# A gated mix of windowed attention and a spatial-gating MLP: where the passes over o, the chunks of wo and VectorE's work for both are issued in the mixing

## The chip, the core and the metric

The kernel runs on one core of a Trainium2 chip. A core has TensorE (PE: matmuls into PSUM), VectorE (DVE), ScalarE (ACT), GpSimd (POOL) and SyncE (SP), each with its own in-order stream of instructions; they meet at semaphores. Data lies in SBUF (128 partitions), matmuls accumulate in eight PSUM banks of 128 x 512 float32, and DMA queues move data between SBUF and memory. SP's queue issues nearly all transfers here; ScalarE's own queue issues a few. The metric is device microseconds of one execution of the whole kernel: the median of several runs, 682.94 us before the change.

## The reference

One input x (2048 x 1024, bf16) goes through two branches, which a per-row gate mixes:

```python
def _A_ref(x, wqkv, wo):          # H = 32 heads of 32, window W = 8, dilation 2
    qkv = (x @ wqkv).reshape(B, S, 3, H, Dh).transpose(2, 0, 3, 1, 4)
    ...
    logits = jnp.einsum('bhsd,bhswd->bhsw', q, kg) * scale
    logits = jnp.where(mask[None, None, :, :], logits, -1000000000.0)
    attn = _softmax(logits, axis=-1)
    o = jnp.einsum('bhsw,bhswd->bhsd', attn, vg)
    return o.transpose(0, 2, 1, 3).reshape(B, S, D) @ wo

def _B_ref(x, w_in, w_sp, b_sp, w_out):
    z = _gelu(jnp.einsum('bsd,df->bsf', x, w_in))
    z1 = z[..., :Fh].copy()
    z2 = _layernorm(z[..., Fh:], axis=-1)
    g = jnp.einsum('ts,bsf->btf', w_sp, z2) + b_sp[None, :, None]
    return jnp.einsum('bsf,fd->bsd', z1 * g, w_out)

g = _sigmoid((x * gate_w).sum(-1, keepdims=True))
return g * _A_ref(x, A_wqkv, A_wo) + (1 - g) * _B_ref(x, ...)
```

S = 2048, D = 1024, Fh = 1792. Each row of the attention looks at 8 earlier rows, two apart, so the attention is elementwise work on VectorE; the projections, the spatial product with w_sp (2048 x 2048) and the products with wo and w_out are matmuls on TensorE.

## The kernel before

The order of every engine's instructions is written out by hand. A small planner, `beat`, keeps a modelled clock of TensorE: `beat.run(cols)` advances `beat.now` as matmuls are issued, and functions put into its heap with `beat.at(t, fn)` are issued once that clock has passed t, wherever the code then is between two products. Whatever `fn` emits lands at that place in its engine's stream, ahead of all that the code emits later. `beat.vector` is a modelled clock of VectorE.

The stages of TensorE, in order: transposes and projections (q, k, v for eight groups of four heads; z2), z1, then the **mixing** (g = w_sp times the normalised z2, line 858 on), then the product with wo and the product with w_out. VectorE does the windowed attention group by group meanwhile (`attention_steps`), well into the mixing.

**The mixing** is 16 groups (`g_group(n)`, u = n // 2 is a block of 256 rows, n % 2 a half of the columns). Each replaces eight block products by seven on sums and differences of blocks. Two PSUM banks accumulate, and a third, a "seed" bank, is forked from the first with ScalarE. In the order of issue on TensorE:

1. product 1 into `pa`; ScalarE **forks** `pa` into a seed bank (`fork`, L856)
2. product 2 into `pd`; ScalarE copies it out (`keep`, L842: p5)
3. product 3 onto `pa`, which needs the fork's reading to be over; copy out (L844: u2)
4. product 4 onto the seed bank; ScalarE writes it to g (L874)
5. product 5 onto `pa`, which needs the u2 copy; copy out (L844: u3). Then `y_norm(n - 1)`: two passes of absolute sums over the last group's y on ScalarE (L669), which wait for VectorE's product with z1 of that group. VectorE adds p5 and u3 (L848)
6. product 6 onto `pd`, which needs the p5 copy; VectorE adds u2 (L848)
7. product 7 onto `pa`, which needs the u3 copy; ScalarE adds the bias (L883). VectorE multiplies g by z1 (L884)

Behind every even group VectorE scales the next block's rows of w_sp (`scale_rows`, L577) and forms their sums (L581, L582); half a microsecond later on the planner's clock `y_finish` scales y of the block before (L674 to L683), and SP stores it (L625).

Beside this run preparations for the product with wo. The matmuls take float16 with power-of-two scales, which need absolute sums:
- `o_norm(g)` (L483): one ScalarE pass over the 128 x 2048 tile `obuf` of the attention group's result, **in place**, so it follows `store_o`, the DMA that reads `obuf` (L428). The last one, in `attended`, writes elsewhere.
- `wo_norm(m)` (L643): one ScalarE pass over a chunk of wo (128 x 768), then the issue of the next chunk's load on ScalarE's own queue (L639), as there is one chunk buffer. Eleven chunks.
- `w_total`, `w_power`, `o_total`, `o_power` (L648 to L659, L486 to L498): small VectorE steps that turn the sums into powers of two, with one tiny matmul each (L655, L492).
- `wo_scale`, `wo_sum` (L513, L518) and `heads_sums(u)` (L503 to L507): VectorE scales wo and the transposed heads of o and forms their sums.

All of these were put into the planner's heap with times of their own. Before the first group three matmuls write the two seed banks (`rest`, L827), so that later products may accumulate onto what ScalarE puts there.

Of the kernel before, what the change touches and what calls it, by code (L numbers as in the profile page):

```python
# [10 lines left out]
F32 = mybir.dt.float32  # L11
# [4 lines left out]
P = 128  # L16
S = 2048
D = 1024
KT = D // P
# [10 lines left out]
ZC = 448  # L30
# [31 lines left out]
def kernel(  # L62
# [367 lines left out]
    def attention_steps(t):  # L430
        beat.at(t - 8.0, lambda: load_qk(0))
        beat.at(t - 7.9, lambda: load_v(0))
        for g in range(NG):
# [8 lines left out]
            if g == 0:  # L442
                t += 5.0
            else:
                for took, fn in pv_steps(g - 1, 0) + pv_steps(g - 1, 1):
                    yield t, took, fn
                t = beat.vector
                beat.at(t + 1.0, lambda g=g: load_v(g))
                beat.at(t + 1.5, lambda g=g: store_o(g - 1))
                beat.at(t + 10.0, lambda g=g: o_norm(g - 1, obuf))  # L450
# [6 lines left out]

    def attended():
# [5 lines left out]
        beat.at(t + 6.0, o_total)  # L464
        beat.at(t + 9.0, o_power)
        plan_heads(0, t + 5.0, 3.0, t + 16.0)
        plan_heads(1, t + 11.0, 3.0)
        for m in range(4):
            beat.at(t + 10.5 + 1.0 * m, lambda m=m: wo_scale(m))
            beat.at(t + 17.5 + 1.5 * m, lambda m=m: wo_sum(m))  # L470
# [50 lines left out]
    prep = {"at": 1e12, "normed": 0, "done": False, "attended": False, "heads": 0}  # L521
# [303 lines left out]
    rest = [seeded.tile([P, 512], F32, name="rest", tag="sd") for _ in range(2)]  # L825
    for r in (0, 1, 0):
        nc.tensor.matmul(rest[r][:], ident[:], mask[:], start=True, stop=True)  # L827
# [31 lines left out]
    def g_group(n):  # L859
# [7 lines left out]
        product(pa, v.a11, b11, f0, f1, True)  # L867
        pb = fork(pa, ZC, lo)
        product(pd, v.s1, t1, f0, f1, True)
# [4 lines left out]
        nc.scalar.copy(g[:, 0, 0], pb[:, 0:ZC])  # L874
        product(pa, v.s3, t3, f0, f1, False)
# [9 lines left out]
        beat.on_vector(1.1)  # L885
        if n + 2 < 2 * NU:
            soon(("z1", n + 2), lambda: load_z1(n + 2))
# [28 lines left out]
    for m in range(11):  # L916
        beat.at(beat.now + 12.0 + 8.0 * m, lambda m=m: wo_norm(m))
    beat.at(beat.now + 3.0, lambda: load_wo_chunk(0))
    beat.at(beat.now + 98.0, w_total)
    beat.at(beat.now + 106.0, w_power)  # L920
    for n in range(2 * NU):
# [16 lines left out]
        if n == 2 * NU - 3:  # L938
            beat.at(beat.now + 0.5, lambda: heads_sums(1))
            plan_heads(2, beat.now + 1.0, 3.0, beat.now + 13.0)  # L940
            plan_heads(3, beat.now + 7.0, 3.0, beat.now + 2 * 7 * KT * ZC * BEAT + 0.5)
    assert prep["attended"]
# [173 lines left out]
```

## Time and profile before

| | |
|---|---|
| median of 3 runs | 682.94 us (681.83 to 683.23) |
| the profiled execution | 681.58 us, span 679.8 us |
| TensorE matmuls busy | 669.3 us |
| VectorE busy | 550.2 us |
| ScalarE busy | 393.9 us |
| the mixing on TensorE | from 368.31 us (group 0) to about 542.7 us |

Rows of a timeline are: start in us from the span's start, duration in us, engine, line of the kernel, operation, what it writes and reads, how many in a row, and in brackets the idle time just before it with what ended it. A matmul's duration reaches from its start to its modelled end, past the start of the next one, so distances are measured from start to start. In a list of waits a row is: who waited, for whom, and then us in total, times, longest us. ACTq and SPq are the queues on which an engine issues transfers.

### The profile page before, as it was taken

The page shows a single profiled execution, that of the slowest core. Times are in us where ns is not written, and L with a number is a line of the kernel's source. Part 1 is how long each engine was busy: PE and PEld are TensorE (multiplying, and loading weights), DVE is VectorE, ACT ScalarE, POOL GpSimd, SP SyncE. Part 2 cuts the span into 40 slices and gives each one's busy share as a digit, 9 for nine tenths or more (in the row PEclk, how much of TensorE's full clock was granted, in tenths as well). Part 3 has the DMA queues.
Part 4 walks back from the last instruction along what each step waited for, and adds up shares of the span by engine and source line. Part 5 has one row for each costly group of instructions (what it writes and reads, how often), then busy time and mean ns, then how long its engine had stood idle before and what let it go on. Part 6 is the DMA issues. An engine that isn't in the chain of part 4 may idle for free. (4 is left out here: it accounts for less than half of the span.)

```text
span 679.8 us, 9533 instructions
## 1 busy us (share of the span) xinstructions
PE 669.3 (98%) x3590; PEld 391.8 (58%) x3590; DVE 550.2 (81%) x628; ACT 393.9 (58%) x736; POOL 13.1 (2%) x23
## 2 busy tenths in 40 slices
PE   9999999999999999999999999989999999999997
PEld 4577788888875555555554555544555444444443
DVE  0009799999999999999999999979956988945745
ACT  4445667665646888858963666655564564522121
POOL 1000000000000000013100000000000000000000
PEclk9999999999999999999999999999999999999999
DMA  8999769998759760437754856494679599385211
GB/s 233 176 232 231 215 183 272 241 259 215 200 121 267 280 199 13 185 102 213 272 170 159 181 144 179 114 273 119 151 209 262 124 254 264 81 171 142 60 63 62
DMA packets 230734, 123.92 MB, mean 182 GB/s; under 512 B 191008, under 2 KB 217248, under 8 KB 230688
## 3 DMA queue, kind: packets, MB, share of 16 engines
q1 hardware_dynamic: 229104, 121.21, 68.1%
q10 hardware_dynamic: 1584, 2.10, 1.1%
q8 instruction: 28, 0.46, 0.3%
q14 instruction: 18, 0.15, 0.1%
HBM read 63.97 MB, written 37.82 MB: 150 GB/s over the span
## 5 line engine op out<-in xcount | busy, mean ns | idle before, releaser
L832 PE MATMUL ps<-arena 128*128 128x448 f16 (+1 forms) x1296 | 264.8, 363 | 4.5 <-ACT seed L856 4.4
L832 PEld LDWEIGHTS <-arena 128*128 128x128 f16 x1512 | 147.7, 98 | 159.6 <-issue 5.7
L713 PEld LDWEIGHTS <-arena 128*128 128x128 bf16 x1024 | 141.6, 138 | 25.6 <-issue 0.8
L713 PE MATMUL ps<-arena 128*128 128x384 bf16 x768 | 130.4, 326 | 0.4 <-DMA arena<-in_A_wqkv_dram 0.4
L374 DVE TENSOR_TENSOR arena<-arena 128x8192 bf16<-128x8192 bf16 x16 | 70.8, 4422 | 46.4 <-DMA arena<-k_d 46.2
L377 DVE TENSOR_TENSOR arena<-arena 128x4096 bf16<-128x4096 bf16 (+1 forms) x64 | 77.6, 1213 | 2.0
L351 PE MATMUL ps<-arena 128*128 128x448 bf16 (+1 forms) x384 | 76.8, 353 | 0.3 <-ACT arena L338 0.3
L351 PEld LDWEIGHTS <-arena 128*128 128x128 bf16 x512 | 49.9, 98 | 46.8 <-ACT arena L338 0.4
L814 PEld LDWEIGHTS <-arena 128*128 128x128 bf16 x512 | 50.0, 98 | 46.6
L814 PE MATMUL ps<-arena 128*128 128x448 bf16 x384 | 75.4, 352 | 0.0
L407 DVE TENSOR_TENSOR arena<-arena,att_A 128x8192 bf16<-128x8192 bf16 x16 | 70.7, 4421 | 0.2
L721 ACT CAST arena<-ps 128x384 bf16<-128x384 f32 x84 | 38.9, 483 | 41.4 <-PE ps L713 37.5
L832 PE MATMUL seed<-arena 128*128 128x448 f16 (+1 forms) x216 | 47.8, 363 | 0.0
L713 PE MATMUL sd<-arena 128*128 128x384 bf16 x256 | 46.8, 326 | 0.0
L357 ACT ACTIVATE arena<-ps 128x448 bf16<-128x448 f32 x48 | 26.1, 546 | 21.7 <-PE ps L351 21.2
L413 DVE TENSOR_TENSOR arena<-arena 128x4096 bf16<-128x4096 bf16 x16 | 36.6, 2290 | 0.4
L1047 ACT ACTIVATE arena<-ps,omr 128x512 f32<-128x512 f32 x24 | 16.5, 687 | 32.4 <-PE ps L832 32.4
L844 ACT ACTIVATE arena<-ps,bt 128x448 f32<-128x448 f32 x32 | 20.3, 633 | 25.4 <-PE ps L832 25.0
L816 ACT ACTIVATE arena<-ps 128x448 bf16<-128x448 f32 x48 | 24.9, 550 | 16.3 <-PE ps L814 14.9
L990 DVE SCALAR_TENSOR_TENSOR arena<-seed,omr,arena 128x512 bf16<-128x512 f32 x8 | 6.0, 751 | 34.5 <-PE seed L832 34.5
L669 ACT ACTIVATE arena<-arena 128x896 bf16<-128x896 bf16 x32 | 30.3, 946 | 3.9 <-DVE arena L884 3.4
L547 ACT ACTIVATE arena<-arena 128x2048 bf16<-128x2048 bf16 x16 | 30.8, 1925 | 0.0
(144 smaller groups left out, 628.5 us busy)
## 6 DMA issues: line engine op xcount, KB each, us to landing
arena<-in_B_w_sp_dram SPq DMA_DIRECT2D x16, 512.0 KB, 5.1
arena<-k_d SPq DMA_DIRECT2D x8, 960.0 KB, 6.6
arena<-v_d SPq DMA_DIRECT2D x8, 960.0 KB, 6.7
z_d<-arena SPq DMA_DIRECT2D x16, 448.0 KB, 2.8
arena<-z_d SPq DMA_DIRECT2D x16, 448.0 KB, 3.9
y_d<-arena SPq DMA_DIRECT2D x16, 448.0 KB, 3.8
arena<-in_A_wqkv_dram SPq DMA_DIRECT2D x24, 256.0 KB, 5.3
arena<-in_B_w_in_dram SPq DMA_DIRECT2D x6, 896.0 KB, 7.7
```

The source lines that it names most:

```text
L351: nc.tensor.matmul(ps[:, 0:N], xT[:, kt, i * P:(i + 1) * P], w2[:, kt, ZC * c:ZC * c + N], start=(kt == 0), stop=(kt == KT - 1))
L357: nc.scalar.activation(z2[:, i, ZC * c:ZC * (c + 1)], ps[:, 0:ZC], ACT.Gelu_apprx_tanh, accum_out=s1[:, 4 * i + c:4 * i + c + 1])
L374: TT(prod.rearrange("p (w j c) -> p w j c", w=W, j=8, c=C), in0, in1, ALU.mult)
L377: return lambda: TT(pv[:, :, 0:half], pv[:, :, 0:half], pv[:, :, half:2 * half], ALU.add)
L407: TT(prod.rearrange("p (w j d h) -> p w j d h", w=W, j=8, d=DH, h=HG), in0, in1, ALU.mult)
L413: return [(4.4, mul), (2.3, lambda: TT(p3[:, 0:4, :], p3[:, 0:4, :], p3[:, 4:8, :], ALU.add)), (1.2, lambda: TT(p3[:, 0:2, :], p3[:, 0:2, ...
L547: nc.scalar.activation(waste, slot, ACT.Abs, accum_out=l1[:, a:a + 1])
L669: nc.scalar.activation(waste, g_ring[n % 4][:, r], ACT.Abs, accum_out=yl[:, k:k + 1])
L713: nc.tensor.matmul(ps[:, 0:3 * C].rearrange("p (t c) -> p t c", t=3), lhsT, wgt[:, 0:3, kt, :], start=(kt == 0), stop=(kt == KT - 1))
L721: nc.scalar.copy(st[:, j % 4, :], ps[:, 0:3 * C])
L814: nc.tensor.matmul(ps[:, 0:ZC], xT[:, kt, i * P:(i + 1) * P], w1[:, kt, :], start=(kt == 0), stop=(kt == KT - 1))
L832: nc.tensor.matmul(ps[:, 0:c1 - c0], w[:, k, :], v[:, k, c0:c1], start=(first and k == 0), stop=(k == K - 1), skip_group_check=True)
```

## The change

Nothing is computed differently and no instruction of an engine is added or taken away; what changes is where they are issued.

- `o_norm` of attention groups that finish in the mixing goes into a list `beside_fork`, and is issued right behind a group's fork, the first one whose time is past (12 us behind its step). Outside the mixing it stays in the heap, with 17 instead of 10 us.
- The `wo_norm` chunks go into `beside_copy`: at most one per group, right behind the copy of product 4 (L874).
- `o_total`, `o_power`, `w_total`, `w_power`, `wo_scale`, `wo_sum`, `heads_sums(0)` and `heads_sums(1)` go into `behind_mult`, a list with a time and a cost each, from which a group takes steps behind its product with z1 (L884), up to 5.0 us of cost (7.4 from group 13 on).
- `heads_sums(2)` and `(3)` stay in the heap with other times.
- The three `rest` matmuls come behind product 1 of group 0 instead of ahead of it.

```diff
@@ -447,7 +447,10 @@
                 t = beat.vector
                 beat.at(t + 1.0, lambda g=g: load_v(g))
                 beat.at(t + 1.5, lambda g=g: store_o(g - 1))
-                beat.at(t + 10.0, lambda g=g: o_norm(g - 1, obuf))
+                if prep["mixing"]:
+                    beside_fork.append((t + 12.0, lambda g=g: o_norm(g - 1, obuf)))
+                else:
+                    beat.at(t + 17.0, lambda g=g: o_norm(g - 1, obuf))
             yield t, 2.3, soft_b
             t = beat.vector
         for took, fn in pv_steps(NG - 1, 0) + pv_steps(NG - 1, 1):
@@ -455,19 +458,27 @@
         t = beat.vector
         beat.at(t + 1.0, attended)
 
+    beside_fork, beside_copy, behind_mult = [], [], []
+
+    def spare(queue):
+        if queue and queue[0][0] <= beat.now:
+            queue.pop(0)[1]()
+
     def attended():
         store_o(NG - 1)
         load_wo()
         o_norm(NG - 1, reg(A_OFF + 8192, 2048).rearrange("p (j c) -> p j c", j=NJ))
         prep["attended"] = True
         t = max(beat.now, beat.vector)
-        beat.at(t + 6.0, o_total)
-        beat.at(t + 9.0, o_power)
-        plan_heads(0, t + 5.0, 3.0, t + 16.0)
+        plan_heads(0, t + 5.0, 3.0)
         plan_heads(1, t + 11.0, 3.0)
+        behind_mult.append((t + 4.0, 0.4, o_total))
+        behind_mult.append((t + 12.0, 0.9, o_power))
         for m in range(4):
-            beat.at(t + 10.5 + 1.0 * m, lambda m=m: wo_scale(m))
-            beat.at(t + 17.5 + 1.5 * m, lambda m=m: wo_sum(m))
+            behind_mult.append((t + 11.0, 0.75, lambda m=m: wo_scale(m)))
+        behind_mult.append((t + 15.0, 2.45, lambda: heads_sums(0)))
+        for m in range(4):
+            behind_mult.append((t + 17.0, 1.25, lambda m=m: wo_sum(m)))
 
     def load_heads(u, r):
         a = 2 * u + r
@@ -518,7 +529,7 @@
         TT(out_, a, b, ALU.subtract)
         beat.on_vector(1.25)
 
-    prep = {"at": 1e12, "normed": 0, "done": False, "attended": False, "heads": 0}
+    prep = {"at": 1e12, "normed": 0, "done": False, "attended": False, "heads": 0, "mixing": False}
 
     def vector_steps(t):
         for item in attention_steps(t):
@@ -822,9 +833,12 @@
                                        ap=[[FH, P], [P * FH, 4], [1, ZC]]), z1s)
     assert prep["done"]
     beat.lead = MIX_LEAD
-    rest = [seeded.tile([P, 512], F32, name="rest", tag="sd") for _ in range(2)]
-    for r in (0, 1, 0):
-        nc.tensor.matmul(rest[r][:], ident[:], mask[:], start=True, stop=True)
+    prep["mixing"] = True
+
+    def wake_seeded():
+        rest = [seeded.tile([P, 512], F32, name="rest", tag="sd") for _ in range(2)]
+        for r in (0, 1, 0):
+            nc.tensor.matmul(rest[r][:], ident[:], mask[:], start=True, stop=True)
 
     def product(ps, w, v, c0, c1, first):
         K = v.shape[1]
@@ -865,13 +879,17 @@
         now(("z1", n), ("y", u - 2))
         pa, pd = [psum.tile([P, 512], F32, name="ps", tag="ps") for _ in range(2)]
         product(pa, v.a11, b11, f0, f1, True)
+        if n == 0:
+            wake_seeded()
         pb = fork(pa, ZC, lo)
+        spare(beside_fork)
         product(pd, v.s1, t1, f0, f1, True)
         p5 = keep(pd, None)
         product(pa, v.s2, t2, f0, f1, False)
         u2 = keep(pa, lo)
         product(pb, v.a12, b21, f0, f1, False)
         nc.scalar.copy(g[:, 0, 0], pb[:, 0:ZC])
+        spare(beside_copy)
         product(pa, v.s3, t3, f0, f1, False)
         u3 = keep(pa, hi)
         if n > 0:
@@ -883,6 +901,10 @@
         nc.scalar.activation(g[:, 1, 0], pa[:, 0:ZC], ACT.Identity, bias=hi)
         TT(g, g, z, ALU.mult)
         beat.on_vector(1.1)
+        room = 5.0 if n < 13 else 7.4
+        while behind_mult and behind_mult[0][0] <= beat.now and room > 0:
+            room -= behind_mult[0][1]
+            behind_mult.pop(0)[2]()
         if n + 2 < 2 * NU:
             soon(("z1", n + 2), lambda: load_z1(n + 2))
 
@@ -914,10 +936,10 @@
     for n in range(2):
         load_z1(n)
     for m in range(11):
-        beat.at(beat.now + 12.0 + 8.0 * m, lambda m=m: wo_norm(m))
+        beside_copy.append((beat.now + 10.0, lambda m=m: wo_norm(m)))
     beat.at(beat.now + 3.0, lambda: load_wo_chunk(0))
-    beat.at(beat.now + 98.0, w_total)
-    beat.at(beat.now + 106.0, w_power)
+    behind_mult.append((beat.now + 115.0, 0.5, w_total))
+    behind_mult.append((beat.now + 122.0, 0.6, w_power))
     for n in range(2 * NU):
         u, fb = n // 2, n % 2
         t = beat.now
@@ -936,10 +958,12 @@
                 fn()
             beat.on_vector(2.8)
         if n == 2 * NU - 3:
-            beat.at(beat.now + 0.5, lambda: heads_sums(1))
-            plan_heads(2, beat.now + 1.0, 3.0, beat.now + 13.0)
-            plan_heads(3, beat.now + 7.0, 3.0, beat.now + 2 * 7 * KT * ZC * BEAT + 0.5)
-    assert prep["attended"]
+            behind_mult.append((0.0, 2.45, lambda: heads_sums(1)))
+            plan_heads(2, beat.now + 1.0, 3.0, beat.now + 2 * 7 * KT * ZC * BEAT + 0.5)
+            plan_heads(3, beat.now + 7.0, 3.0, beat.now + 2 * 7 * KT * ZC * BEAT + 3.5)
+    assert prep["attended"] and not beside_fork and not beside_copy
+    while behind_mult:
+        behind_mult.pop(0)[2]()
 
     t = beat.now
     beat.at(t + 5.0, lambda: y_norm(2 * NU - 1))
```

In the built program the first `o_norm` of the mixing, which was put into the heap ahead of the mixing, moves from group 0 (behind L874) to group 1 (behind the p5 copy, L842); the next one moves from between L669 and L883 of group 7 to right behind the fork of group 8; the last one stays behind the fork of group 12. A chunk stands behind L874 in each of groups 1 to 11. `w_total` is issued behind group 10's L884, `w_power` behind group 11's, `o_total` behind group 12's; `o_power`, `wo_scale`, `heads_sums(0)` and the first `wo_sum` behind group 13's; the other three `wo_sum` and `heads_sums(1)` behind group 14's; `heads_sums(2)` and `(3)` behind group 15's. The order on SP and GpSimd is the same as before.

## The prediction

> **What bounds the kernel now.** I read the page's busy list first, then the list of waits of TensorE, then TensorE's timeline through the mixing, then the timelines of ScalarE and VectorE around each place where TensorE stood.
>
> ```profile
> PE 669.3 (98%) x3590; PEld 391.8 (58%) x3590; DVE 550.2 (81%) x628; ACT 393.9 (58%) x736; POOL 13.1 (2%) x23
> ```
> ```profile
> PE ps L832 <- ACT seed L856: 4.4, 2, 3.4
> ```
>
> TensorE is the bound: 98% busy, and its two waits on the fork (L856) are the only large ones in the mixing. A change that adds and removes no matmul, like this one, can only move such waits. The timeline gives their true size, since a stall is the distance of two starts beyond the work between them:
>
> ```profile
> 365.51 1.68 PE L814 MATMUL sd<-arena 128*128 128x448 bf16 x8
> 367.02 0.38 PE L827 MATMUL rest<-mask,ident 128*128 128x512 bf16 x1
> 367.88 0.59 PE L827 MATMUL rest<-mask,ident 128*128 128x512 bf16 x2 [0.48 <-ACT arena L816]
> 368.31 4.70 PE L832 MATMUL ps<-arena 128*128 128x448 f16 x24
> 372.84 1.68 PE L832 MATMUL seed<-arena 128*128 128x448 f16 x8
> 374.36 9.42 PE L832 MATMUL ps<-arena 128*128 128x448 f16 x48
> 383.62 1.68 PE L832 MATMUL seed<-arena 128*128 128x448 f16 x8
> ...
> 394.21 1.68 PE L832 MATMUL seed<-arena 128*128 128x448 f16 x8
> ...
> 404.80 1.68 PE L832 MATMUL seed<-arena 128*128 128x448 f16 x8
> ...
> 448.69 7.73 PE L832 MATMUL ps<-arena 128*128 128x448 f16 x40
> 459.80 1.67 PE L832 MATMUL ps<-arena 128*128 128x448 f16 x8 [3.38 <-ACT seed L856]
> ...
> 526.44 7.73 PE L832 MATMUL ps<-arena 128*128 128x448 f16 x40
> 535.16 1.67 PE L832 MATMUL ps<-arena 128*128 128x448 f16 x8 [1.00 <-ACT seed L856]
> ```
>
> From one seed row to the next (383.62 to 394.21) a group of seven products takes 10.59 us, so a product takes 1.513. I write P1 to P7 for a group's products; the seed row is P4. Measured with that:
> - Before P1 of group 0: three wake-up matmuls at 0.215 each (367.88 to 368.31 are two) would let P1 start at 367.02 + 0.65 = 367.67; it starts at 368.31. **0.64 us.**
> - Group 0 behind P4: 383.62 - 374.36 = 9.26 against 6 x 1.513 = 9.08. **0.18 us**, hidden inside a busy row.
> - P3 of group 8: 448.69 + 5 x 1.513 = 456.26, but it starts at 459.80. **3.54 us.**
> - P3 of group 15: 526.44 + 7.57 = 534.01, but it starts at 535.16. **1.15 us.**
>
> Together 5.51 us; that is the most that the change can win here. What held ScalarE in group 8 stands in its timeline:
>
> ```profile
> 455.38 1.91 ACT L483 ACTIVATE arena<-arena 128x2048 bf16<-128x2048 bf16 x1 [2.34 <-DMA o_d<-arena]
> ...
> 457.29 0.83 ACT L643 ACTIVATE arena<-arena 128x768 bf16<-128x768 bf16 x1
> ...
> 458.62 0.63 ACT L883 ACTIVATE arena<-ps,bt 128x448 bf16<-128x448 f32 x1 [0.41 <-ACT arena L643]
> 459.15 0.60 ACT L856 ACTIVATE seed<-ps,bt 128x448 f32<-128x448 f32 x1
> ```
>
> The pass over o (L483, in place, so it waits until o's store has landed) and a chunk pass (L643) stand ahead of group 7's last bias (L883) and of group 8's fork (L856), whose reading of the bank P3 needs. For group 15 the chain begins on VectorE:
>
> ```profile
> 459.29 1.09 DVE L884 TENSOR_TENSOR arena<-arena 128x1792 bf16<-128x1792 bf16 x1 [4.60 <-ACT arena L883]
> ...
> 517.14 1.23 DVE L577 TENSOR_TENSOR arena<-arena,rs_b 128x2048 f16<-128x2048 bf16 x1 [0.79 <-DMA arena<-in_B_w_sp_dram]
> ...
> 522.99 0.15 DVE L493 TENSOR_SCALAR var<-ps 128x8 f32<-128x8 f32 x1
> ...
> 526.40 0.62 DVE L848 TENSOR_TENSOR arena<-arena 128x448 bf16<-128x448 f32 x1
> ...
> 530.86 1.08 DVE L884 TENSOR_TENSOR arena<-arena 128x1792 bf16<-128x1792 bf16 x1
> ```
> ```profile
> 531.97 0.95 ACT L669 ACTIVATE arena<-arena 128x896 bf16<-128x896 bf16 x1 [3.19 <-DVE arena L884]
> ```
>
> The first row belongs to group 7 and is used below. From 517.14 on: rows of w_sp landed late, then o's and wo's small work (L493 onward) ran ahead of group 13's product with z1 (L884), which group 14's y pass (L669) on ScalarE waited for, with group 15's fork queued behind it.
>
> **The change, part by part.**
>
> *The wake-up matmuls behind P1 of group 0.* Same three matmuls; P1 uses a bank that was free long ago, and by its end the last gelu has gone. The 0.64 us go. Group 0's fork now takes the bank that the third of them wrote, 0.65 us after P1; P2's 1.513 us cover that and the fork's 0.60. Bounds: gain 0 to 0.64; I take 0.64, as nothing else is late there.
>
> *The pass over o that stood in group 0* was already in the due queue before the mixing began and only moves from 10 to 17 us behind its step: in the built order it stands in group 1, between the copy of P2 and the copy of P3. In group 0 it stood in the same way between two copies:
>
> ```profile
> 373.05 0.63 ACT L844 ACTIVATE arena<-ps,bt 128x448 f32<-128x448 f32 x1 [0.98 <-PE ps L832]
> 374.56 0.53 ACT L874 CAST arena<-seed 128x448 bf16<-128x448 f32 x1 [0.88 <-PE seed L832]
> 374.99 1.91 ACT L483 ACTIVATE arena<-arena 128x2048 bf16<-128x2048 bf16 x1
> ...
> 376.89 0.62 ACT L844 ACTIVATE arena<-ps,bt 128x448 f32<-128x448 f32 x1
> ```
>
> Copy, 1.90 us of pass, copy, then the product two further on: 376.89 plus 0.67 is P7's start (374.36 + 3.03 + 0.18 = 377.57). The shape is the same, so the 0.18 us are gained in group 0 and paid again in group 1: net 0 (bounds -0.18 to +0.18). The other passes over o move by 7 us in earlier stages; TensorE waits for no such pass there in the list of its waits, so 0.
>
> *Chunks of wo behind the copy of P4, one per group from group 1.* From the copy to the next copy with a chunk between: 0.43 (374.56 to 374.99) + 1.35 (403.92 to 405.27 below). The u3 copy so starts 0.20 + 1.78 = 1.98 us after P5 starts, and P7 can start 0.67 later, at 2.65; it is due at 3.03. A margin of 0.38 us in each of eleven groups, so 0, except in group 3, where the exponential's pass sits ahead of the P4 copy:
>
> ```profile
> 396.35 0.85 ACT L643 ACTIVATE arena<-arena 128x768 bf16<-128x768 bf16 x1
> ...
> 403.92 0.85 ACT L643 ACTIVATE arena<-arena 128x768 bf16<-128x768 bf16 x1
> ...
> 405.27 0.63 ACT L844 ACTIVATE arena<-ps,bt 128x448 f32<-128x448 f32 x1 [0.41 <-PE ps L832]
> 405.92 1.28 ACT L392 ACT_TABLE_LOAD   x1
> 407.21 0.63 ACT L392 ACTIVATE att_L<-att_L 128x512 f32<-128x512 f32 x1
> ...
> 408.16 0.64 ACT L844 ACTIVATE arena<-ps,bt 128x448 f32<-128x448 f32 x1
> ```
>
> Before, the chunk stood ahead of the u2 copy (L844 at 405.27), where there was room. After: P4 starts at 404.80 - 0.64 = 404.16, the u2 copy 0.21 later (373.05 against 372.84) at 404.37, then 2.89 (405.27 to 408.16) for table, exponential and P4 copy, 1.35 for the chunk: the u3 copy starts at 408.61 and P7 at 409.28 instead of 404.16 + 4.54 = 408.70. **A new stall of 0.58 us** (bounds 0.3 to 0.8: the phase against before is known to some 0.2 us).
>
> The Trainium skill, "ScalarE: Activation LUTs", section "What ACT_TABLE_LOAD costs", says that a switch costs a load of about 1283 ns and a drain of about 1380 ns more. The trace shows the load at 1.28 us and the exponential 0.01 us behind it, with no drain in between; by the page this stall would be 1.96 us and the whole gain 3.37, by the row it stays at 0.58.
>
> *The pass over o in group 8 goes behind the fork.* TensorE is then 0.64 - 0.58 = 0.06 us ahead of before, so P1 of group 8 starts at 456.26 - 3.03 - 0.06 = 453.17, and its fork 0.21 behind P2's start like the copies (454.89), on time. The pass can start when the fork is through, 0.6 later, 455.5. Its store:
>
> ```profile
> 446.24 0.59 SPq L428 DMA_DIRECT2D o_d<-arena  x1
> ```
> ```profile
> o_d<-arena SPq DMA_DIRECT2D x1, 512.0 KB, 9.1
> ```
> ```profile
> o_d<-arena SPq DMA_DIRECT2D x8, 512.0 KB, 6.5
> ```
>
> (the issue; its landing time; the median of all eight.) It lands at 446.24 + 9.1 = 455.34. SP's order is unchanged, so I leave it there. The pass ends at 457.4, the p5 copy at 457.9, the u2 copy starts at 457.9, where it is due anyway. P5 (459.22) is held only if the pass starts later than 459.22 - 0.67 - 0.53 - 1.90 = 456.12: a margin of 0.6. All 3.54 us are won; bounds 1.5 (a store 2.7 us late) to 3.54. The last pass (group 12) stays where it was.
>
> *VectorE's work handed out behind L884.* No operation is added. Behind the rows of w_sp come, in the built order, their sums and the y scaling, group 13's two additions and L884, and only then the powers, wo scaling, heads and wo sums. VectorE loses its 4.60 us wait for L883 in group 7 (row 459.29), so SP's transfers behind its steps, the last w_sp rows among them, come with TensorE about 3.5 us earlier (an estimate: 3.54 + 0.06 less a tenth). From 517.14 to 522.99 are 5.85 us; so the additions begin at 517.14 - 3.5 + 5.85 = 519.5, and L884, 1.08 long with two additions before it (L848, 0.62 each at most), ends at 521.8. Group 14's y pass wants it about 0.75 after P6's start, at 526.44 + 1.51 - 3.60 + 0.75 = 525.1: 3.3 us of room. If the rows came no earlier, L884 would end at 525.3, 0.2 late for a y pass that itself has room. So the 1.15 us go (bounds 0.5 to 1.15).
>
> What was ahead of L884 is late next: heads, sums and group 15's work end in
>
> ```profile
> 548.23 0.42 DVE L507 TENSOR_TENSOR arena<-arena 128x512 f16<-128x512 f16 x1
> 550.78 0.75 DVE L990 SCALAR_TENSOR_TENSOR arena<-ps,g_s,arena 128x512 f32<-128x512 f32 x1 [2.13 <-PE ps L832]
> ```
>
> VectorE runs without a gap from 517.14 to 548.65, with the same work after the change, so it ends at 545.15; the first finish (L990) is wanted at 550.78 - 4.75 = 546.03. It fits with 0.9 us; with rows that come no earlier it would be up to 2.6 us late. I take 0. The two one-off matmuls (powers of wo and o) now follow P7 of groups 11 and 13; their inputs come from VectorE some 8 us earlier by the same reckoning: 0.
>
> **The sum.** 0.64 + 0.18 + 3.54 + 1.15 - 0.18 - 0.58 = 4.75 us. The profiled execution took 681.58 us (span 679.8, 1.78 around it), so 676.83 by its own measure. It stands 1.36 below the median of the runs, 682.94; against that median, **678.2 us**.
>
> **The rivals.**
> - *The store of o lands late and ScalarE now waits behind the fork instead of ahead of it.* For it: this store took 9.1 us against 6.5 in the median of all eight, and only 0.6 us are free. Against: no transfer is added, and a wo chunk that was issued beside it now comes later. Price: landing minus 456.12; at 458.0 it is 1.9 us, 680.1.
> - *VectorE's work moved back is late in the wo product.* If the w_sp rows keep their old time, up to 2.6 us return at the first finish: 680.8. Against: they are issued behind VectorE's and TensorE's own steps, both earlier.
> - *Slower: the chunk behind the P4 copy.* ScalarE's in-order queue makes u3, and so P7, wait for the chunk's pass and for the issue of the next chunk. It decides once that gap is more than 1.35 + 0.38 us. With a gap of 2.4 us, 0.67 us come back in each of eleven groups, 7.4 in all: 678.2 + 7.4 = 685.6. For it: in the built program that issue also waits for earlier transfers of SP's queue. Against: a chunk stood behind the P4 copy in group 2 already (396.35), and from that group's P4 to the next (394.21 to 404.80) are 10.59 us, no stall.
> - *It doesn't do what it says:* a pass misses its fork by its due time and goes back ahead of it. The built order shows it behind the fork in group 8, so I give it nothing of its own.
>
> **How the numbers follow.** Forecast 0.70, late store 0.11, late VectorE 0.11, chunk 0.05, others 0.03. The forecast's own range is from 682.94 - 5.51 - 1.1 (the lowest run is that much under the median) = 676.3 to 678.2 + 1.1 = 679.3; the late cases draw the upper end to 680.6, and 676.2 is the lower. A difference under 0.2% (1.4 us) can't be told from none. Faster than 681.6 hold the forecast and nearly all of the two late cases, 0.91; within 0.2% 0.04; slower 0.05.
>
> **What would show it.** Right: no TensorE wait on L856 of over 0.2 us; distances of 10.6 us from one seed row to the next, but about 10.8 from group 1's and 11.2 from group 3's; P1 of group 0 following the last gelu product at once; the group 8 pass over o directly behind the fork with a wait under 0.6 us; L669 of group 14 not waiting for L884. Wrong: a wait of P5 on L844 in group 8; idle VectorE replaced by TensorE waits on L990 after the mixing; many groups of over 10.7 us.

## The result and the profile after

| | before | after |
|---|---|---|
| median | 682.88 us (681.83 to 683.38, 6 runs) | 679.13 us (678.56 to 681.61, 6 runs) |
| ratio | | 0.9951, 95% interval 0.9935 to 0.9968 |
| the profiled execution | 681.58 us, span 679.8 | 679.4 us, span 677.6 |

The changed kernel is faster by 3.75 us. Its code has moved: in the fences below `o_norm` is L494, `wo_norm` L654, the fork L870, the copies L856, L858 and L891, the bias L901, the passes over y L680, the mixing's products L846, the wo product's finish L1014, the gelu of z1 L827.

TensorE's list of waits (who waited, for whom, total us, times, longest us) no longer has the fork:

```profile
...
PE ps L825 <- ACT arena L827: 0.7, 1, 0.7
PE ps L724 <- DMA arena<-in_A_wqkv_dram: 0.6, 1, 0.6
PE ps L846 <- DVE arena L1014: 0.6, 1, 0.6
PE ps L846 <- ACT arena L858: 0.5, 1, 0.5
```

TensorE's timeline of the kernel after, through the mixing:

```profile
367.25 1.68 PE L825 MATMUL sd<-arena 128*128 128x448 bf16 x8
368.77 1.68 PE L846 MATMUL ps<-arena 128*128 128x448 f16 x8
...
373.95 1.68 PE L846 MATMUL seed<-arena 128*128 128x448 f16 x8
...
384.55 1.68 PE L846 MATMUL seed<-arena 128*128 128x448 f16 x8
...
395.32 1.68 PE L846 MATMUL seed<-arena 128*128 128x448 f16 x8
...
405.92 1.68 PE L846 MATMUL seed<-arena 128*128 128x448 f16 x8
...
411.10 6.21 PE L846 MATMUL ps<-arena 128*128 128x448 f16 x32 [0.48 <-ACT arena L858]
417.15 1.68 PE L846 MATMUL seed<-arena 128*128 128x448 f16 x8
...
448.93 1.68 PE L846 MATMUL seed<-arena 128*128 128x448 f16 x8
...
459.52 1.68 PE L846 MATMUL seed<-arena 128*128 128x448 f16 x8
...
523.13 1.68 PE L846 MATMUL seed<-arena 128*128 128x448 f16 x8
...
533.73 1.68 PE L846 MATMUL seed<-arena 128*128 128x448 f16 x8
...
544.96 1.89 PE L846 MATMUL seed<-arena 128*128 128x512 f16 x8
```

From seed row to seed row: 10.60 us in group 0, 10.77 from group 1's, 11.23 from group 3's, 10.59 over group 8's fork (it was 14.13), 10.60 over group 15's (11.75). From the last z1 row with `sd` to the first wo seed are 177.71 us; before, from 365.51 to 548.07, 182.56. **The mixing gained 4.85 us.** ScalarE's timeline in group 8 shows the new order, fork, pass over o without a wait, copies on time:

```profile
456.70 0.61 ACT L870 ACTIVATE seed<-ps,bt 128x448 f32<-128x448 f32 x1 [0.88 <-PE ps L846]
457.23 1.90 ACT L494 ACTIVATE arena<-arena 128x2048 bf16<-128x2048 bf16 x1
...
459.12 0.52 ACT L856 COPY arena<-ps 128x448 f32<-128x448 f32 x1
459.72 0.63 ACT L858 ACTIVATE arena<-ps,bt 128x448 f32<-128x448 f32 x1
```

But the profiled execution gained only 2.18 us. Two new waits account for most of the difference. One lies in the z1 stage, ahead of the mixing (TensorE, then ScalarE, kernel after):

```profile
317.80 1.68 PE L825 MATMUL sd<-arena 128*128 128x448 bf16 x8
...
321.74 3.19 PE L825 MATMUL ps<-arena 128*128 128x448 bf16 x16 [0.75 <-ACT arena L827]
324.76 1.68 PE L825 MATMUL sd<-arena 128*128 128x448 bf16 x8
```
```profile
311.12 0.98 ACT L827 ACTIVATE arena<-ps 128x448 bf16<-128x448 f32 x2 [8.62 <-DMA z_d<-arena]
...
317.59 1.90 ACT L494 ACTIVATE arena<-arena 128x2048 bf16<-128x2048 bf16 x1
...
321.16 0.96 ACT L827 ACTIVATE arena<-ps 128x448 bf16<-128x448 f32 x2
```

The same pass in the timeline of the kernel before:

```profile
308.78 1.91 ACT L483 ACTIVATE arena<-arena 128x2048 bf16<-128x2048 bf16 x1 [7.01 <-DMA o_d<-arena]
```

In both kernels ScalarE stands idle here for 7 to 9 us, until late transfers have landed. Before, the pass over o was in that hole; 7 us later on the planner's clock it comes behind the hole, into the backlog, and holds the gelu that TensorE's next bank needs. Two `sd` distances of 6.05 grew to 6.96 and 6.17: **1.02 us lost.** Its size varies: the six kernels here with the 17 us lose 0.3 to 1.0 us in this place, the eight with 10 us nothing. The other wait is in the wo product (TensorE, VectorE and SP's queue of the kernel after):

```profile
569.47 1.89 PE L846 MATMUL seed<-arena 128*128 128x512 f16 x8
...
575.39 7.07 PE L846 MATMUL ps<-arena 128*128 128x512 f16 x32 [0.58 <-DVE arena L1014]
582.29 1.89 PE L846 MATMUL seed<-arena 128*128 128x512 f16 x8
```
```profile
569.95 0.75 DVE L514 TENSOR_SCALAR arena<-arena,var 128x2048 f16<-128x2048 bf16 x1 [3.98 <-DMA arena<-o_d]
...
572.21 2.47 DVE L985 TENSOR_SCALAR arena<-arena,wsc 128x1792 f16<-128x1792 bf16 x4
```
```profile
539.55 1.10 SPq L636 DMA_DIRECT2D y_d<-arena  x2
540.74 8.66 SPq L485 DMA_TRANSPOSE arena<-o_d  x6
...
562.84 4.64 SPq L485 DMA_TRANSPOSE arena<-o_d  x2
```

The same place in VectorE's timeline of the kernel before:

```profile
570.75 0.75 DVE L503 TENSOR_SCALAR arena<-arena,var 128x2048 f16<-128x2048 bf16 x1 [1.83 <-DMA arena<-o_d]
```

VectorE waits 3.98 us for the last heads instead of 1.83, scales w_out (L985), and only then reaches the finish that empties TensorE's bank. The distance is 12.82 where it was 12.09: **0.73 lost.** Together with 0.72 of loads and projections at the start and 0.18 at the end: -4.85 + 0.72 + 1.02 + 0.73 + 0.18 = -2.2 us, the difference of the spans.

The 0.72 at the start are not the change's: they are there at the first projection, which follows a load (21.36 us before, 22.08 after), and the first pass over o runs at 132 us and later. The start varies by itself. The last `sd` row, less the z1 stall, stands at 366.23 here, at 365.7 to 367.4 in the twelve kernels below, and at 365.51 before, the earliest of all.

Part of why the medians differ by 3.75 and these two executions by 2.18 came out with the fourth experiment.

### The profile page after: what moved, and what is told of

Same layout as the page of the kernel before. It is cut to its first block, busy times and chain, and to the rows that moved or that the text cites. A ratio compares the mean times of both kernels' runs of the same rounds, so it can differ in the third digit from the quotient of the medians.

```text
span 677.6 us, 9538 instructions
## 1 busy us (share of the span) xinstructions
PE 670.0 (99%) x3590; PEld 392.5 (58%) x3590; DVE 550.5 (81%) x628; ACT 394.1 (58%) x736; POOL 13.1 (2%) x23
## 4 chain that ended last, share of the span: by engine, by line
PE 80%; DVE 10%; SPq 3%; DMA 3%; ACT 2%; issue 1%; ACTq 0%; DVEq 0%
PE ps L846 36%; PE ps L724 18%; PE sd L724 6%; PE seed L846 6%; PE ps L825 5%; PE ps L351 5%; DVE arena L407 2%; PE sd L825 2%; PE sd L351 2%; SPq L709 1%; DVE arena L377 1%; DVE arena L374 1%; DMA z_d<-arena 1%; DVE arena L413 1%; DMA arena<-o_d 1%
## 5 line engine op out<-in xcount | busy, mean ns | idle before, releaser
L846 PE MATMUL ps<-arena 128*128 128x448 f16 (+1 forms) x1296 | 264.8, 363 | 1.1 <-DVE arena L1014 0.6
L846 PEld LDWEIGHTS <-arena 128*128 128x128 f16 x1512 | 147.7, 98 | 156.3 <-issue 2.4
L846 PE MATMUL seed<-arena 128*128 128x448 f16 (+1 forms) x216 | 47.8, 363 | 0.0
L827 ACT ACTIVATE arena<-ps 128x448 bf16<-128x448 f32 x48 | 24.9, 552 | 24.4 <-PE ps L825 13.7
L1014 DVE SCALAR_TENSOR_TENSOR arena<-seed,omr,arena 128x512 bf16<-128x512 f32 x8 | 6.0, 751 | 34.5 <-PE seed L846 34.5
L858 ACT ACTIVATE arena<-ps,bt 128x448 f32<-128x448 f32 x32 | 20.3, 634 | 21.9 <-PE ps L846 19.8
L680 ACT ACTIVATE arena<-arena 128x896 bf16<-128x896 bf16 x32 | 30.2, 945 | 0.5
```

The source lines that it names most:

```text
L680: nc.scalar.activation(waste, g_ring[n % 4][:, r], ACT.Abs, accum_out=yl[:, k:k + 1])
L846: nc.tensor.matmul(ps[:, 0:c1 - c0], w[:, k, :], v[:, k, c0:c1], start=(first and k == 0), stop=(k == K - 1), skip_group_check=True)
```

## The experiments

Each time stands beside runs of the kernel before on the same chip. Those had medians of 682.86 to 683.08 us beside e1 to e8, and 681.0 to 681.4 beside e9 to e12, where ratios are compared. Every kernel has line numbers of its own; the text beside a fence says what its rows are.

**e1: what the passes outside the mixing cost.** The kernel after, with

```diff
-                    beat.at(t + 17.0, lambda g=g: o_norm(g - 1, obuf))
+                    beat.at(t + 10.0, lambda g=g: o_norm(g - 1, obuf))
```

> The changed kernel with one thing undone: the passes over o outside the mixing are due 10 us behind their step again, not 17. Theory A (the 7 us cost time): in the z1 stage the pass runs while ScalarE waits for z's store anyway, instead of adding its 1.9 us to the backlog behind it; TensorE's wait for the gelu in the z1 stage (0.75 us idle, 1.02 us from start to start) goes, and the time falls by 1.0 us, to about 678.1. Rival B (the late store of z alone holds ScalarE for 8.6 us and causes that stall): the stall stays, time as the changed kernel, 679.1. In the mixing the first pass stands in group 0 again: 0.18 us lost there instead of in group 1.

Measured: 678.65 us (677.91 to 679.0), ratio 0.9933 [0.9917, 0.9949]. ScalarE's timeline has the pass back in the hole:

```profile
309.35 1.91 ACT L494 ACTIVATE arena<-arena 128x2048 bf16<-128x2048 bf16 x1 [6.92 <-DMA o_d<-arena]
```

All `sd` distances are 6.05 or 6.06 again, so the z1 loss hangs on that delay; the time alone can't show 1 us, as the intervals of this ratio and the changed kernel's overlap. TensorE comes earlier and the wo product gives some of it back: 13.36 instead of 12.82. Group 0 pays 0.18 again, as expected, but group 1 doesn't get it back (10.79).

**e2: the pass over o behind the fork, alone.** The kernel before, with

```diff
-                beat.at(t + 10.0, lambda g=g: o_norm(g - 1, obuf))
+                if prep["mixing"]:
+                    beside_fork.append((t + 12.0, lambda g=g: o_norm(g - 1, obuf)))
+                else:
+                    beat.at(t + 10.0, lambda g=g: o_norm(g - 1, obuf))
...
         pb = fork(pa, ZC, lo)
+        spare(beside_fork)
```

> The kernel before with one part of the change: the pass over o of group 8 behind the fork. Theory A: the stall of group 8 (3.54 us) goes whole, although the chunk of wo still stands ahead of that fork; group 15's stall of 1.15 us stays, as VectorE's order is the old one; the 0.64 us ahead of the mixing and 0.18 us in group 0 stay: 682.9 - 3.5 = 679.4. Rival B (the fork needs the chunk moved too): 1.0 to 1.4 us of the stall stay, 680.6. Rival C (the store of o lands late and P5 of group 8 waits instead): some us of stall at P5, time over 681.

Measured: 678.68 us (677.94 to 679.31), ratio 0.9936 [0.992, 0.9953]. Group 8's distance is 10.59, group 15 keeps its stall (11.83), z1 and wo product have none. This part alone brings as much as the whole change. Its store was issued at 446.56 and took 9.4 us, to 455.96; the fork ran at 455.74 and the pass at 456.27, so the late-store rival's wait was 0.3 us away.

**e3: the chunks behind the copy, alone.** The kernel before, with

```diff
         nc.scalar.copy(g[:, 0, 0], pb[:, 0:ZC])
+        spare(beside_copy)
...
-        beat.at(beat.now + 12.0 + 8.0 * m, lambda m=m: wo_norm(m))
+        beside_copy.append((beat.now + 10.0, lambda m=m: wo_norm(m)))
...
-    beat.at(beat.now + 98.0, w_total)
-    beat.at(beat.now + 106.0, w_power)
+    beat.at(beat.now + 124.0, w_total)
+    beat.at(beat.now + 132.0, w_power)
```

> The kernel before with one part of the change: the chunks of wo behind the copy of product 4 (with the power of wo due a little later than the last chunk). Theory A: the chunk's 1.33 us no longer stand between the pass over o and the fork of group 8, so 3.54 us of stall become 2.2; in group 3 a new stall of 0.58 us before product 7, none in the other groups: net 682.9 - 1.3 + 0.6 = 682.2. Rival B (every chunk behind the copy holds product 7): 0.2 us or more in each of eleven groups, 684.3 or above.

Measured: 679.31 us (678.47 to 679.8), ratio 0.9942 [0.9925, 0.9959]. A miss: the pass over o still stands ahead of the fork, yet group 8's distance is 10.65. TensorE's and ScalarE's timelines (products, then the pass over o and the fork):

```profile
450.21 9.30 PE L838 MATMUL ps<-arena 128*128 128x448 f16 x48
```
```profile
454.79 1.89 ACT L489 ACTIVATE arena<-arena 128x2048 bf16<-128x2048 bf16 x1
...
457.19 0.59 ACT L862 ACTIVATE seed<-ps,bt 128x448 f32<-128x448 f32 x1
```

TensorE's row answers the one at 448.69 before, 1.52 us earlier there; the pass starts 0.59 earlier than at 455.38 and waits for nothing. With the chunk's 1.33 that makes 3.44 of the 3.54. Of the 1.52, 0.64 are group 3's new stall and 0.88 a later start. So a stall here is the distance between two clocks, TensorE's and that of the pass over o, which follows the store or, where that has landed, ScalarE's own queue; whatever moves either changes it. e10 to e12 test that.

**e4: VectorE's work behind the product, alone.** The kernel before, with `behind_mult`, all its steps, and `heads_sums(2)` and `(3)` as in the change:

```diff
         beat.on_vector(1.1)
+        room = 5.0 if n < 13 else 7.4
+        while behind_mult and behind_mult[0][0] <= beat.now and room > 0:
+            room -= behind_mult[0][1]
+            behind_mult.pop(0)[2]()
```

> The kernel before with one part of the change: VectorE's work for o and wo behind each group's product with z1. Theory A: of the stalls only group 15's 1.15 us goes; group 8 keeps 3.54 us: 682.9 - 1.15 = 681.7. Rival B (the stall of group 15 goes only because the transfers come earlier once group 8 is mended): 682.9. Rival C (VectorE's end of the mixing is late in the wo product): a wait of TensorE for a finish in the wo product grows from 0.34 us by 0.5 or more.

Measured: 682.29 us (681.05 to 685.7), ratio 0.9992 [0.9977, 1.0008]: nothing gained. Group 15's stall is gone (10.60), but the third distance of the wo product is 14.54, 2.45 more than before: nearly the 2.6 of the prediction's second rival, but not at the first finish, which is in time (12.42, as before), and with VectorE waiting for the last heads:

```profile
575.28 0.75 DVE L511 TENSOR_SCALAR arena<-arena,var 128x2048 f16<-128x2048 bf16 x1 [5.70 <-DMA arena<-o_d]
```

This execution shows something else as well. TensorE's timeline in group 8 (products; L864 is the fork), and its table of stretches (stretch, its length, PE busy with matmuls, granted clock, DMA share, GB/s):

```profile
449.71 7.73 PE L840 MATMUL ps<-arena 128*128 128x448 f16 x40
459.94 2.96 PE L840 MATMUL ps<-arena 128*128 128x448 f16 x8 [2.50 <-ACT seed L864]
462.70 2.11 PE L840 MATMUL seed<-arena 128*128 128x448 f16 x8
464.65 9.24 PE L840 MATMUL ps<-arena 128*128 128x448 f16 x48
```
```profile
460.00:462.00 2.00, 2.00 (x7) 0.54 1.18 245
462.00:464.00 2.00, 2.00 (x8) 0.61 1.06 219
464.00:466.00 2.00, 2.00 (x13) 1.00 1.06 267
```

Behind the stall the granted clock is 0.54 to 0.61 for about 4 us, and two products take 4.71 us instead of 3.03: in this execution the stall costs 1.7 us more than its own length. In the profiled execution of before the clock was 1.00 behind its stall of 3.54 us in the same place, and it was 1.00 here behind the 2.45 us in the wo product.

**e5: the 17 us outside the mixing, alone.** The kernel before, with

```diff
-                beat.at(t + 10.0, lambda g=g: o_norm(g - 1, obuf))
+                beat.at(t + (10.0 if prep["mixing"] or g > 5 else 17.0), lambda g=g: o_norm(g - 1, obuf))
```

> The kernel before with one thing changed: the passes over o outside the mixing are due 17 us behind their step instead of 10. Theory A: the z1 stage grows by about 1.0 us (a wait of TensorE for a gelu), 682.9 + 1.0 = 683.9, and nothing else moves. Rival B (that stall in the changed kernel was chance or another part's): 682.9.

Measured: 682.82 us (681.5 to 685.72), ratio 0.9998 [0.9984, 1.0013]: no difference in time, so the price of e1 isn't confirmed by it. The z1 stage shows the loss smaller (6.26 and 6.17, 0.33 us), and group 8's distance falls by 0.49, 14.13 to 13.64. That the stall takes up the loss in z1 fits this, but isn't shown: this execution also started late, with TensorE 2.17 us and the pass over o 1.68 us later than before.

**e6: the last heads behind w_out.** The kernel after, with

```diff
-        plan_heads(7, beat.now + 0.3, 1.5, beat.now + 17.0)
+        plan_heads(7, beat.now + 0.3, 1.5, beat.now + 19.0)
```

> The changed kernel with VectorE's second scaling of w_out ahead of the sums of the last heads (due 19 instead of 17 us behind the first pair of wo groups). Theory A: in the third pair of the wo product the first finish waits behind that scaling, which waits behind the heads' late transfer; with the order turned the 0.72 us of stall there go: 679.1 - 0.7 = 678.4. Rival B (w_out lands as late as the heads): VectorE ends both at the same time, stall and time as before, 679.1.

Measured: 678.45 us (677.72 to 681.95), ratio 0.9948 [0.9934, 0.9963]. The third distance is 12.09, the z1 loss (0.97) stays. The expected time came, though 0.7 us is less than the interval can tell; the distance shows it.

**e7: each chunk's pass twice**, the price of a late u3 copy. The kernel after, with

```diff
-        nc.scalar.activation(w_chunk[:, 0:n], w_chunk[:, 0:n], ACT.Abs, accum_out=s2[:, m:m + 1])
+        for _ in range(2):
+            nc.scalar.activation(w_chunk[:, 0:n], w_chunk[:, 0:n], ACT.Abs, accum_out=s2[:, m:m + 1])
```

> The changed kernel with every chunk's absolute-sum pass done twice in a row: 0.97 us more ScalarE work behind the copy of product 4 in groups 1 to 11. Theory A (margin of 0.38 us before product 7): 0.97 - 0.38 = 0.59 us in each of ten groups and 0.97 in group 3, 6.9 us in all, 686.0, each seen as a wait of TensorE for the u3 copy. Rival B (there is more slack than the sum says): under 2 us in all, 681.

Measured: 685.88 us (684.97 to 687.88), ratio 1.0053 [1.0037, 1.007]. The distances are 11.25 in nine groups (0.66 more) and 12.21 in group 3 (0.98 more), 6.9 us in all; group 11, whose chunk is the short last one (128 x 512), has no stall (10.62). TensorE's list of waits, for the u3 copy:

```profile
PE ps L847 <- ACT arena L859: 5.7, 10, 1.4
```

The margin of 0.38 us and the price of 0.67 per group in the prediction's third rival hold, though for ten groups rather than eleven; its condition did not occur.

**e8: the mendings together.** The kernel after with e1's and e6's edits, the first pass of the mixing also behind a fork, and chunks in groups 0 to 2 and 4 to 11, so that none meets group 3's exponential:

```diff
-        spare(beside_copy)
+        if n != 3:
+            spare(beside_copy)
```

> The changed kernel with its four leftovers mended: passes outside the mixing due at 10 us, the pass that is due in group 0 put behind the fork of group 1, chunks in groups 0 to 2 and 4 to 11 (none in group 3, where the exponential runs), the second scaling of w_out ahead of the last heads. Theory A: the stalls of 1.02 (z1), 0.17 (group 1), 0.6 (group 3) and 0.72 us (third pair) go, 2.5 us: 679.1 - 2.5 = 676.6. Rival B (the stalls are not additive, what is won comes back at the next late transfer): 677.5 to 678.5.

Measured: **677.14 us (676.76 to 677.96), ratio 0.992 [0.9903, 0.9937]**, the best version, with a span of 675.4 in its profile. That is 2.0 us below the changed kernel where 2.5 were expected. The stalls of group 3, z1 and the third distance (12.09) are gone. One new wait stands in its list, group 2's products for VectorE's sums (the distance from group 1's seed row is 10.98): TensorE has caught up with the next engine.

```profile
PE ps L852 <- DVE arena L598: 0.2, 1, 0.2
```

**e9: y of block 6 first.** The kernel after, with y's power, scaling and store ahead of `behind_mult` in group 14:

```diff
+        if n == 14:
+            y_power(6)
+            y_scale(6)
+            soon(("y", 6), lambda: y_done(6))
         room = 5.0 if n < 13 else 7.4
...
-        if fb == 0 and u > 0:
+        if fb == 0 and 0 < u < NU - 1:
             y_finish(u - 1)
```

> The kernel after, with the power and the scaling of y of block 6 issued directly behind group 14's product with z1, ahead of the three wo sums and the sums of heads 1. Theory A: the third product of the wo stage stalls (its seed distance is 12.82 against 12.09 us) because VectorE's scaling of block 6 ends at 540.2 us, only 1.7 us earlier than in the kernel before, and SP's store of it (539.55), its six transposes of heads (540.74), the loads of w_out and the transposes of heads 7 (562.84) follow one another in SP's queue. Ahead of the sums the scaling ends some 5.5 us earlier, the transposes of heads 7 come at least 1 us earlier, VectorE's wait of 3.98 us ahead of their sums shrinks to under 3 us and the third distance is 12.09 to 12.2: 679.1 - 0.7 = 678.4 us. Theory B (the transposes of heads 7 wait for the w_out loads' own time and not for the place of the store): they issue at 562.8 as before, the distance stays at 12.8 and the time at 679.1. Both: the z1 stall of about 1.0 us stays.

Measured: 678.28 us (677.35 to 679.08), ratio 0.9963 [0.9949, 0.9977]. SP's and VectorE's timelines:

```profile
537.53 7.99 SPq L485 DMA_TRANSPOSE arena<-o_d  x6
...
558.58 4.26 SPq L485 DMA_TRANSPOSE arena<-o_d  x2
```
```profile
565.34 0.75 DVE L514 TENSOR_SCALAR arena<-arena,var 128x2048 f16<-128x2048 bf16 x1
```

The last transposes issue 4.3 us earlier (L485; L514 is the scaling of the last heads), VectorE waits for nothing, the third distance is 12.09. So the 0.73 us came by way of SP's queue, from VectorE's wo sums standing ahead of y's scaling. The time beside another chip's runs can't show 0.7 us.

**e10: one chunk out of group 8's chain.** The kernel before, with the chunk at 457.29 behind the fork; no other instruction moves but the load that it issues:

```diff
-        beat.at(beat.now + 12.0 + 8.0 * m, lambda m=m: wo_norm(m))
+        beat.at(beat.now + 12.0 + 8.0 * m + (4.0 if m == 9 else 0.0), lambda m=m: wo_norm(m))
```

> The kernel before, with the tenth chunk's pass (the one at 457.29 us, ahead of group 7's bias and group 8's fork) 4 us later on the planner's clock, which puts it behind that fork; every other instruction of every engine stays where it was. Theory A (stalls on the fork are sums of what stands ahead of it): the chunk's 1.33 us leave the chain and nothing else does; group 8's distance falls from 14.13 to about 12.8, the pass over o still waits some 2.3 us for its store, and the time is 682.9 - 1.3 = 681.6 us. Theory B (the chunk is what holds group 8, as the kernel with all chunks behind the copy seemed to show with its distance of 10.65): the distance falls to about 10.7 and the time to 679.6 us.

Measured: 679.36 us (678.39 to 681.17), ratio 0.9977 [0.9966, 0.9988], which holds theory A's 0.998 and leaves out B's 0.995. TensorE's and ScalarE's timelines:

```profile
449.47 7.73 PE L832 MATMUL ps<-arena 128*128 128x448 f16 x40
457.99 1.67 PE L832 MATMUL ps<-arena 128*128 128x448 f16 x8 [0.79 <-ACT seed L856]
```
```profile
454.92 1.91 ACT L483 ACTIVATE arena<-arena 128x2048 bf16<-128x2048 bf16 x1 [1.10 <-DMA o_d<-arena]
```

The stall is 457.99 - 449.47 - 7.57 = 0.95. TensorE came 0.78 later than before (448.69) and the pass 0.46 earlier; 3.54 - 0.78 - 0.46 = 2.30, and the chunk's 1.33 leaves 0.97. In an unshifted execution it would by this sum have been 2.2 (an estimate). The chunk is worth its own length; the rest is the two clocks.

**e11 and e12: the same delay ahead of the mixing, with a stall behind it and without.** The kernel before, and e9's, with twelve more wake-up matmuls:

```diff
-    for r in (0, 1, 0):
+    for r in (0, 1) * 7 + (0,):
```

> The kernel before with 15 instead of 3 of the matmuls that write the seed banks, 12 x 0.215 = 2.6 us of TensorE's time more ahead of the mixing's first product, and nothing else. Theory A (what holds group 8, and less so group 15, are moments set by VectorE's attention and the store of o, so a TensorE that comes later waits less there): group 8's distance falls from 14.13 to about 11.6 us, group 15's shrinks too, and the time stays as before within 0.5 us, a ratio of 1.000. Theory B (the stalls are set by ScalarE's queue behind TensorE and move along with it): the distance stays at 14.1 and the time rises by 2.6 us, a ratio of 1.0038.

> The kernel with y of block 6 first (the one after, with that edit), with the same 12 matmuls more ahead of group 0's second product. No stall of its mixing or its wo product waits for VectorE or a store, so nothing takes the 2.6 us up: distances from seed row to seed row as without them, 10.6 us in group 8 and 12.1 in the third wo product, and the time rises from 0.9963 of the kernel before by 0.0038 to about 1.000 of it, which is where the kernel before stands with or without the same delay. Rival (group 3's exponential or a later stall takes up part): under 0.9985.

Measured: e11 682.48 us (681.52 to 683.4), ratio 1.0017 [1.0007, 1.0027], between the theories: by the medians 1.1 of the 2.6 us came through. In its trace group 8's distance is 11.70, theory A's number, but group 15's grew to 12.25: there VectorE's scaling of the late w_sp rows starts 1.73 us later than before (518.87), TensorE only 1.24. In group 8 ScalarE's timeline shows that the store no longer holds the pass over o:

```profile
456.63 1.90 ACT L483 ACTIVATE arena<-arena 128x2048 bf16<-128x2048 bf16 x1
```

TensorE came 3.68 us later than before (the delay and a later start), the fork only 1.25 later: 3.54 - 3.68 + 1.25 = 1.11, the stall that is left. The wait for the store is used up, and these 1.11 us are ScalarE's own queue, pass and chunk behind the y passes, which moves along with TensorE as theory B has it.

e12 681.26 us (680.01 to 683.11), ratio 0.9995 [0.9984, 1.0006]: 0.0032 above e9's, 2.2 us, with all distances behind the delay as in e9 but for 0.07 in group 3; z1's loss ahead of it happened to be 0.4 smaller. With no stall to take it up, the delay goes through; it is the distances that show this, as the intervals of the two times (e11's 0.5 to 1.8 us, e12's about 1 to 3.4) overlap.

## Why the prediction was right, and where it was not

By its steps:

- *Wake-up matmuls, group 0, group 1.* Right: P1 follows the last z1 product at 1.52 us, and group 1 pays 0.17 for the 0.18 of group 0.
- *Group 3.* 0.63 measured, 0.58 predicted. The table load took 1.28 and the exponential followed 0.01 later; the 1.96 that the Trainium skill, "ScalarE: Activation LUTs", "What ACT_TABLE_LOAD costs", would have made of it did not come.
- *Other groups with a chunk.* 10.59 to 10.62: no stall, and e7 prices the margin. The 7.4 us of the third rival counted eleven equal chunks; the last one is shorter, so it should have been ten groups, 6.7.
- *Group 8.* The 3.54 are gone, with no wait for the store. But it is not a sum of parts: e2 and e3 each remove nearly all of it, and e10 and e11 show why. The term was that of one execution's two clocks, in which TensorE started earliest of all; e4, which keeps this stall and started 1.02 us later, has 2.7.
- *Group 15.* Right (10.60 for 11.75), and e4 ties it to VectorE's new order.
- *The sum of the mixing.* 4.85 measured, 4.75 predicted.
- *"The other passes over o move by 7 us in earlier stages; TensorE waits for no such pass there in the list of its waits, so 0."* **Failed**, 1.02 us. The list shows what TensorE waits for now, not what the pass would meet 7 us later. The row that answers it was ScalarE's idle 7.01 us ahead of the pass: work that leaves a hole has to be paid where it lands.
- *"It fits with 0.9 us ... I take 0" for VectorE's end.* **Failed**, 0.73 us. The first finish was in time, as predicted. The step looked only at VectorE's end and not at what its steps release: y's scaling went behind the wo sums, and SP's store and transposes behind that (e9). The rival had the stage and the sign, not the finish nor the way, at a fourth of its 2.6 us; e4 has nearly that size at the same third pair.
- *"It stands 1.36 below the median of the runs; against that median, 678.2 us."* **Failed**, in the other direction: after's profiled execution stands 0.27 above its median. The offset was not a constant of measurement. The sum also took a stall's price to be its length, which e4's products behind the stall don't bear out.

These errors nearly cancel: 1.02 + 0.73 + 0.72 (the start) + 0.18 (the end) - 0.10 (the mixing) - 1.63 (the offset) = 0.92, the distance from 678.2 to 679.13 but for rounding. The forecast's direction and its main term were right; that its time came so near is partly chance.

## What the runs showed of the hardware

Part of the offset belongs to the stall. Of the 83 executions of the kernel before that ran beside the experiments, 47 have a mean granted clock of 0.998 or less, the other 36 of 0.999 or 1.0. On the three chips the first kind has medians of 682.18, 683.23 and 683.60 us, the second of 680.58, 681.79 and 682.46: 1.1 to 1.6 us apart. In the kernels whose longest stall in the mixing is under 1.7 us (after, e1 to e3, e6 to e12), 1 of 88 executions has such a clock; in e4, with 2.7 us in its profile, 7 of 12, and in e5, with 3.05, 3 of 12. e10 and e11 differ from before by one moved chunk or by a delay alone and have no stall over 1.7 us: 0 of their 24 executions have a lowered clock, 18 of the 40 of before beside them. e4's table of stretches shows where it lies: the products right behind the stall.

The Trainium skill, "TensorE: Matmul & The Clock Gate", Part 1, says that TensorE falls to half its clock after about one idle window of 3.4 us, and that the windows run freely. e4's 0.54 and 0.61 for about 4 us fit the level, but its 2.50 us idle are shorter than the window; here the measurement decides. Free windows could explain why some executions are hit and others with the same stall are not; only one such execution was traced, so this is argued, not shown.

The full-clock executions of before have medians 0.5 to 1.1 us under the median of all that ran beside them. So the clock may account for that much of the 1.36 us; of the six executions of before that the result rests on no clock is known. The rest lies within the spread of full-clock executions (681.42 to 683.08 us on one chip). The stall that the change removed was thus worth 3.5 us in the profiled execution, less where TensorE starts later, and in over half of the others it cost some 1.1 to 1.7 more than its length.

A second thing: a stall that waits for another engine's or a transfer's clock takes up delays ahead of it. In e11 the mixing's largest stall shrank by 2.4 us behind the delay, and the 2.6 us cost 1.1 by the medians (1.7 against the runs of before beside it with a full clock, since none of e11's twelve has a lowered one); in e12, without such a stall, no distance shrank. It may also be why e5's loss in z1 can't be seen in the time, and why, once the mixing's stalls were gone, small new ones (L1014, L598) came to light.

## What to carry to other kernels

Price a moved instruction at the place where it arrives, and look there for what is queued behind it, on its own engine and on the queues that its results release; a zero taken from today's list of waits is no price. Where a stall comes from two independent clocks, its parts don't add and its size in one profile is one draw; read both clocks' rows and the granted clock right behind it. An offset between the profiled execution and the median may itself be part of what the change removes, so compare the mean granted clock of the runs before carrying it over.
